# Query loads in rows of 1024 bytes, with two schedules reordered, in a retention kernel followed by a low-rank mixer

## The chip, the cores and the metric

The kernel runs on one core of one Trainium2 chip. The metric is the device time of one execution in microseconds; lower is better. A core has a matrix engine (TensorE, "PE" in the profile, with its weight loads as "PEld"), a vector engine (DVE), an activation engine (ACT), a general engine (POOL) and a small engine whose queue issues DMAs (SP). Each takes its instructions in the order in which the program gave them; semaphores let one wait for another. Sixteen DMA engines move the data of all queues.

## The reference

Four batches (B), eight heads (H), 768 tokens (S), 64 numbers to a head (D). A recurrent attention with a decay per head is followed by a mixer: a low-rank mixing of the tokens (rank 32), then an MLP of 512 -> 2048 -> 512.

```python
gamma = 1.0 - 2.0 ** (-5.0 - np.arange(H, dtype=np.float32))
scale = 1.0 / np.sqrt(D)
for t in range(S):
    state = gamma[None, :, None, None] * state + np.einsum('bhd,bhe->bhde', k[:, :, t], v[:, :, t])
    y[:, :, t] = scale * np.einsum('bhd,bhde->bhe', q[:, :, t], state)
...
x = np.ascontiguousarray(attn_out.transpose(0, 2, 1, 3)).reshape(B, S, H * D)
...
h = xt @ U @ V                      # xt: x with tokens and features exchanged
u = x + h.transpose(0, 2, 1)
ch = np.maximum(u @ w_ch1, 0.0) @ w_ch2
return (u + ch).astype(np.float32)
```

## The kernel before, in words

**Attention in chunks.** The recurrence is turned into matrix products. A chunk has 128 tokens, so a batch has six (NCK). Scores of a chunk are k times q, masked to the past; outputs are masked scores times v plus q times the state of the chunks before. The decay enters as factors exp(position x log gamma): positive powers go with q, negative ones with k or v. `gq`, `gk` hold them one token to a partition, `gq2`, `gk2` two tokens to a partition. The factor of q can be put on q when it is cast to bf16, or on the output x.

**Batch 0 and its units.** Batch 0 works in six units: unit u has four heads (g = 0 or 1) and 256 tokens (one of three blocks). `load_heads` (line 105) brings a unit in with two neighbouring tokens on each partition: for each partition and head a row of 2 x 64 x 4 = 512 bytes. The loads are issued on SP in the order of the list in line 115, and land in a ring of 20 buffers (`ring`, line 97). What happens to them is an order written out by hand, `STEPS`: K0, Q0, V0 are the casts to bf16 of unit 0, Tk0 and Tq0 the transposes on TensorE (as matmuls with the identity), kT0 and qT0 their way out of PSUM, S0 the scores, m0 the mask, ST0.0 a chunk's addition to the state and s0.0 its copy, M0 the mix, x0 the output; FTk1:3 are three matmuls with zeros that keep TensorE busy. `BY` says for each unit which engine (A, D, P for ACT, DVE, POOL) does a step, whether q is `scaled` in its cast, and whether the negative power goes on k (`ks` = 1) or v. If q is not scaled, `x_out` multiplies on DVE. The last steps (xt, P, pc, E, N, R, u, B) are the low-rank mixing and the first MLP matmuls (`begin_up`, line 400).

**Weights.** The step w0 makes POOL copy one element of the last q unit (line 746, the gate), so that the first quarter of w1 is loaded only after it; w1 is the second quarter. After `STEPS`, POOL issues the third quarter and, behind `feed_behind(511)`, the fourth, then four loads for w2, and stands before `feed_behind(1023)`. `feed_behind(col)` copies an element of w1 that arrives with the first or second quarter into a ring buffer; SP's next load into that buffer has to wait for it.

**Feed of batches 1 to 3.** `feed` lists the loads in order; `feed_more` issues them while ring buffers are free and `n_open` allows: two at first, six behind the first gate, the rest of batch 1 behind the second. k and v of batch 1 come one token to a partition, in rows of 256 bytes; q of batch 1 comes like batch 0's units.

**MLP passes with the next batch woven in.** `mlp_pieces(b)` gives a batch's MLP as pieces: 16 up-projections of 512 tokens (line 429), 8 of the other 256 tokens for two blocks each (line 442), then the down-projections (line 458). Each up-projection fills one of three PSUM banks called `mlp`, and a relu on ACT or, every third time, on DVE empties it (lines 420 and 418). `weave` emits the pieces in order and, before them, the steps of the next batch's attention whose mark, a share of the pass, has come: `turn_k1`, `turn_q1` (transposes of batch 1 into `mlp` banks, with an evacuation each), `score`, `mix`, the casts `prep_two`, and the low-rank steps. `score` masks on DVE (line 284), `mix` uses the state from `nsz`. Outputs are stored from POOL's queue (line 408).

## Time and profile before

| | us |
|---|---|
| median of three runs | 226.52 |
| the three runs | 229.25, 224.36, 226.52 |
| the profiled execution | 223.51 |
| its span, first to last instruction | 221.7 |
| TensorE busy in the span | 216.1 |
| matmuls of line 458 / 429 / 442 | 88.1 / 56.8 / 29.6 |
| relus on ACT (line 420) / DVE (line 418) | 38.1 / 22.1 |

The profile was taken in one execution. A busy time is the sum of an engine's instructions, and a group's mean is that of one instruction. The chain is followed back from the last instruction: at each step to what released it, or to the instruction before it on its engine. In timelines the columns are the start, the time taken, the engine, line, operation, and output and input with partitions x elements; in brackets the idle time before it and what ended it. Where the DMA engines and TensorE stand in the span's 40 equal slices of 5.5 us:

```profile
DMA  5999999999999996789896644411112530001112
GB/s 163 317 303 253 189 219 203 195 217 229 306 261 263 279 269 108 166 174 211 168 295 167 174 122 97 95 43 31 47 52 88 152 95 0 0 3 47 72 70 96
DMA packets 89381, 34.58 MB, mean 156 GB/s; under 512 B 71216, under 2 KB 87856, under 8 KB 89360
```

The DMA engines are busy in 9 tenths or more of the first 80 us or so, TensorE nearly everywhere.

### The profile page before, as it was taken

How to read it: one execution, taken by the hardware profiler on the slowest of the kernel's cores; microseconds unless marked ns; L12 is line 12 of the kernel's file. 1: busy time of each engine (PE TensorE's matmuls, PEld its weight loads, DVE VectorE, ACT ScalarE, POOL GpSimd, SP SyncE). 2: the span in 40 equal slices, each digit the busy share in tenths (PEclk: the TensorE clock that was granted, in tenths of full speed). 3: DMA queues.
4: the chain of work that ended last, by engine and by line, in shares of the span. 5: the costliest groups of instructions: out<-in, count | busy, mean ns of one | idle time of the engine just before them, and what ended most of it. 6: DMA issues, size and time to landing. Idle time of an engine off the chain costs nothing.

```text
span 221.7 us, 4773 instructions
## 1 busy us (share of the span) xinstructions
PE 216.1 (97%) x1982; PEld 122.9 (55%) x1982; DVE 96.7 (44%) x137; ACT 82.6 (37%) x157; POOL 79.3 (36%) x114
## 2 busy tenths in 40 slices
PE   7999999999999999999999999999999999999994
PEld 2567444775665544588454444587454444774442
DVE  6578546226445266526336144443525242221121
ACT  3676354454554134484230034746030044430000
POOL 5589473126760059390100498530101000000110
PEclk9999999999999999999999999999999999999999
DMA  5999999999999996789896644411112530001112
GB/s 163 317 303 253 189 219 203 195 217 229 306 261 263 279 269 108 166 174 211 168 295 167 174 122 97 95 43 31 47 52 88 152 95 0 0 3 47 72 70 96
DMA packets 89381, 34.58 MB, mean 156 GB/s; under 512 B 71216, under 2 KB 87856, under 8 KB 89360
## 3 DMA queue, kind: packets, MB, share of 16 engines
q1 hardware_dynamic: 83296, 24.06, 47.1%
q0 software_dynamic: 6064, 10.23, 18.6%
q8 instruction: 15, 0.25, 0.4%
q14 instruction: 6, 0.05, 0.1%
HBM read 27.46 MB, written 6.29 MB: 152 GB/s over the span
## 4 chain that ended last, share of the span: by engine, by line
PE 87%; SPq 6%; DMA 5%; issue 0%; ACT 0%; DVE 0%; POOL 0%
PE mlp L458 38%; PE mlp L429 25%; PE mlp L442 13%; SPq L106 5%; DMA w1b<-in_moe_w_ch_dram 3%; PE r L281 2%; PE r L302 2%; DMA in<-in_q_dram 2%; PE r L297 2%; PE st L313 2%; PE r L344 1%; PE mlp L400 1%; PE mlp L271 1%; PE r L382 0%; SPq L117 0%
## 5 line engine op out<-in xcount | busy, mean ns | idle before, releaser
L458 PE MATMUL mlp<-w2b,gT 128*128 128x512 bf16 (+2 forms) x400 | 88.1, 371 | 0.0
L420 ACT ACTIVATE gT<-mlp 128x512 bf16<-128x512 f32 x64 | 38.1, 597 | 70.2 <-PE mlp L429 57.4
L458 PEld LDWEIGHTS <-gT 128*128 128x128 bf16 x400 | 36.9, 98 | 38.6 <-issue 0.2
L429 PE MATMUL mlp<-uT,w1b 128*128 128x512 bf16 x250 | 56.8, 379 | 0.0
L408 POOL DMA_DIRECT2D out_dram<-o x23 | 12.7, 554 | 103.5 <-DVE o L465 95.8
L418 DVE TENSOR_SCALAR gT<-mlp 128x512 bf16<-128x512 f32 x32 | 22.1, 690 | 46.2 <-PE mlp L429 23.9
L429 PEld LDWEIGHTS <-w1b 128*128 128x128 bf16 x250 | 23.6, 98 | 27.3
L465 DVE TENSOR_TENSOR o<-mlp,u 128x512 f32<-128x512 f32 (+2 forms) x25 | 16.8, 670 | 45.0 <-PE mlp L458 44.8
L442 PE MATMUL mlp<-uT,w1b 128*128 128x256 bf16 x256 | 29.6, 273 | 0.2 <-ACT gT L420 0.2
L442 PEld LDWEIGHTS <-w1b 128*128 128x128 bf16 x256 | 24.8, 98 | 4.2 <-issue 0.4
L284 DVE TENSOR_TENSOR a<-r,mask 128x1024 bf16<-128x1024 f32 x18 | 21.2, 1219 | 7.0 <-PE r L281 7.0
L83 POOL TENSOR_TENSOR vd<-in,gk 128x512 bf16<-128x512 f32 x18 | 18.7, 1040 | 10.4 <-DMA in<-in_v_dram 10.2
L70 ACT ACTIVATE x<-r 128x512 bf16<-128x512 f32 x20 | 11.9, 596 | 25.9 <-PE r L302 25.6
L351 DVE TENSOR_TENSOR u<-r,x 128x512 bf16<-128x512 f32 (+1 forms) x16 | 14.6, 951 | 3.9 <-PE r L344 3.9
L81 POOL CAST kd<-in 128x512 bf16<-128x512 f32 x16 | 9.7, 611 | 8.0 <-issue 6.2
L83 POOL TENSOR_TENSOR qd<-in,gq 128x512 bf16<-128x512 f32 x12 | 12.5, 1041 | 0.0
L70 ACT ACTIVATE nsz<-st 64x256 bf16<-64x256 f32 x30 | 11.2, 372 | 0.3
L83 POOL TENSOR_TENSOR qp<-in,gq 128x512 bf16<-128x512 f32 x6 | 6.2, 1052 | 5.6 <-DMA in<-in_q_dram 5.6
L591 DVE TENSOR_TENSOR a<-r,mask 128x1024 bf16<-128x1024 f32 x6 | 7.3, 1222 | 2.0 <-PE r L584 2.0
L302 PE MATMUL r<-vd,a 128*128 128x64 bf16 x144 | 7.1, 193 | 0.0
L302 PEld LDWEIGHTS <-a 128*128 128x128 bf16 x144 | 6.0, 98 | 0.7
L297 PEld LDWEIGHTS <-qT 128*128 128x128 bf16 x60 | 4.6, 98 | 2.7
(109 smaller groups left out, 152.2 us busy)
## 6 DMA issues: line engine op xcount, KB each, us to landing
in<-in_k_dram SPq DMA_DIRECT2D x24, 256.0 KB, 4.9
in<-in_q_dram SPq DMA_DIRECT2D x24, 256.0 KB, 4.7
in<-in_v_dram SPq DMA_DIRECT2D x24, 256.0 KB, 4.8
out_dram<-o POOLq DMA_DIRECT2D x23, 256.0 KB, 2.3
w1b<-in_moe_w_ch_dram POOLq DMA_DIRECT2D x4, 512.0 KB, 8.7
w2b<-in_moe_w_ch_dram POOLq DMA_DIRECT2D x4, 512.0 KB, 15.8
kT<-kd SPq DMA_TRANSPOSE x12, 2.4
qT<-qd SPq DMA_TRANSPOSE x12, 2.4
```

The lines of the kernel that those rows point to most:

```text
L70: nc.scalar.activation(dst, src, AF.Copy)
L83: e.tensor_tensor(dst, src, scale, op=ALU.mult)
L284: nc.vector.tensor_tensor(a, r.rearrange("p i (n m) -> p i n m", n=4), mask[:, None, None, :].to_broadcast([P, 2, 4, P]), op=ALU.mult)
L302: nc.tensor.matmul(o[:, ts(h, D)], a[:, i, hp], vb[:, h], start=(ci == 0 and h == 0), stop=True, skip_group_check=True)
L351: nc.vector.tensor_tensor(v4(us[b][:, ds(j0, nj), e]), R[g][:, :, :nj * P].rearrange("p c (j e) -> p c j e", j=nj), v4(xs[b][:, ds(j0, nj) ...
L408: eng.dma_start(out=dst, in_=src)
L418: nc.vector.tensor_relu(dst, src)
L420: nc.scalar.activation(dst, src, AF.Relu)
L429: nc.tensor.matmul(g_p[:, :sz], w1b[:, c, ts(m, P)], uTs[b][:, c, ds(lo, sz)], start=(c == 0), stop=(c == NCB - 1))
L442: nc.tensor.matmul(g_p[:, ts(n, S - LO)], w1b[:, c, ts(m + n, P)], uTs[b][:, c, LO:], start=(c == 0), stop=(c == NCB - 1))
L458: nc.tensor.matmul(ch[:, :nn], gT[:, m, ts(j, P)], w2b[:, m, ds(n0, nn)], start=(m == 0), stop=(m == NM - 1))
L465: nc.vector.tensor_tensor(o_sb, ch[:, :nn], us[b][:, j, n], op=ALU.add)
```

## The change

q of batches 0 and 1 is loaded with four neighbouring tokens on a partition, in rows of 1024 bytes. A q unit is now one of three parts of a group g of four heads: parts 0 and 1 hold two heads and 512 tokens each, part 2 holds four heads and the last 256 tokens, in two loads of 64 partitions. A score unit therefore needs two q units (0 and 1, or 3 and 4) or part 2 alone. The transposed q of a whole batch goes to one tile (`qT0`, or the one of batch 1), written with a step of four elements. q of batch 0 is no longer scaled in its cast, so all six outputs x are multiplied on DVE, and `gq2` goes. Batch 1's q is scaled by new constants `g4`, made by `q4_consts`, which is called after `feed_behind(1023)`. The order of batch 0's loads, its `BY` and its `STEPS` are new; so are the feed's order for q of batch 1 and the marks of its transposes and of its first k casts.

```diff
+    Q4 = 512
+    def load_q4(t, b, i):
+        g, part = divmod(i, 3)
+        if part < 2:
+            nc.sync.dma_start(
+                out=t.rearrange("p (h x) -> p h x", h=2),
+                in_=q[b, ds(HG * g + 2 * part, 2), ds(0, Q4), :].rearrange(
+                    "h (t j) d -> t h (j d)", j=4))
+            return
+        for n in range(2):
+            nc.sync.dma_start(
+                out=t[ds(64 * n, 64)].rearrange("p (h x) -> p h x", h=2),
+                in_=q[b, ds(HG * g + 2 * n, 2), ds(Q4, S - Q4), :].rearrange(
+                    "h (t j) d -> t h (j d)", j=4))
...
-    for step in ("k0 q0 v0 k1 q1 v1 k2 q2 v2 k3 q3 v3 k4 q4 U k5 q5 v4 v5 ").split():
+    for step in ("k0 q0 q1 v0 k1 v1 k2 q2 v2 k3 q3 q4 v3 k4 U k5 q5 v4 v5 ").split():
...
-    feed = [(nm, 1, 2 * pp + n) for pp in range(NCK // 2) for nm in "kqv"
-            for n in range(2)]
+    QS = ((0, 1, 3, 4), (), (2, 5))
+    feed = [(nm, 1, ci) for pp in range(NCK // 2) for nm in "kqv"
+            for ci in (QS[pp] if nm == "q" else (2 * pp, 2 * pp + 1))]
...
-    gq2 = consts.tile([P, NB, H, 2], fp32)
-    nc.scalar.activation(gq2, pos2, AF.Exp)
...
-    nc.vector.tensor_scalar(gq2, gq2, 1.0 / math.sqrt(D), None, op0=ALU.mult)
...
+    g4 = consts.tile([P, H + 4, 4], fp32)
+    def q4_consts():
+        pa, pc = ramp([P, H, 4], [[0, H], [1, 4]], 4), ramp([P, 4, 4], [[0, 4], [1, 4]], 4, Q4)
+        nc.vector.tensor_scalar(pc[ds(64, 64)], pc[ds(64, 64)], -256.0, None, op0=ALU.add)
+        nc.vector.tensor_tensor(
+            g4[:, :H], pa, lgt[:, :, None].to_broadcast([P, H, 4]), op=ALU.mult)
+        lgv = lgt.rearrange("p (g n h) -> p n g h", n=2, h=2)
+        for n in range(2):
+            r = ds(64 * n, 64)
+            nc.vector.tensor_tensor(
+                g4[r, H:].rearrange("p (g h) j -> p g h j", g=2),
+                pc[r].rearrange("p (g h) j -> p g h j", g=2),
+                lgv[r, n, :, :, None].to_broadcast([64, 2, 2, 4]), op=ALU.mult)
+        nc.scalar.activation(g4, g4, AF.Exp)
+        nc.vector.tensor_scalar(g4, g4, 1.0 / math.sqrt(D), None, op0=ALU.mult)
...
+    def cast_q4(eng, b, i, src, scaled):
+        t = rpre.tile([P, 4, 2, D], bf16, tag="qd", name=f"q4_{b}_{i}")
+        cast(eng, t, src.rearrange("p (h j d) -> p j h d", h=2, j=4),
+             scale_q4(i) if scaled else None)
+        return t
+    def turn_q4(tp, t):
+        for j in range(4):
+            nc.tensor.matmul(tp[:, ts(j, P)], t[:, j], ident, start=True, stop=True)
+    def turned_q4(eng, qT, i, tp):
+        g, part = divmod(i, 3)
+        if part < 2:
+            evac(eng, qT[:, 2 * g + part, :Q4].rearrange("p (t j) -> p j t", j=4),
+                 tp.rearrange("p (j t) -> p j t", j=4))
+        else:
+            evac(eng, qT[:, ds(2 * g, 2), Q4:].rearrange("p n (t j) -> p j n t", j=4),
+                 tp.rearrange("p (j n t) -> p j n t", j=4, n=2))
...
     def prep_two(nm, pp, eng="P"):
-        for ci in (2 * pp, 2 * pp + 1):
+        for ci in QS[pp] if nm == "q" else (2 * pp, 2 * pp + 1):
...
-        evac("AD"[g], t[:, ds(2 * g, 2)].rearrange("p n (t j) -> p n j t", j=2),
-             tp.rearrange("p (n j t) -> p n j t", n=2, j=2))
+        tp = bank("mlp")
+        turn_q4(tp, pre.pop(("q", 1, i)))
+        turned_q4("ADADAD"[i], bts["q1"], i, tp)
...
-             "K": "DDPPPP",
-             "Q": "PPDPPA",
-             "scaled": "111000",
-             "ks": "110010",
-             "V": "APPPPP",
-             "kT": "AADAAA",
-             "qT": "AAAAAA",
-             "x": "AADDAD",
+             "K": "DPPPPP",
+             "Q": "ADPPPA",
+             "scaled": "000000",
+             "ks": "101011",
+             "V": "APAPPP",
+             "kT": "DAADAA",
+             "qT": "ADAAAA",
+             "x": "DDDDDA",
...
-        "Va K0 Vb FTk0:1 Q0 Tk0 FTq0:2 Vc V0 Tq0 kT0 ST0.0 FTk1:3 K1 qT0 Tk1 Q1 "
-        "s0.0 S0 kT1 ST0.1 FTq1:1 m0 V1 s0.1 Tq1 qT1 K2 ST1.0 M0 s1.0 S1 Q2 x0 "
-        "ST1.1 Tk2 m1 s1.1 V2 Tq2 FTk3:2 qT2 K3 ST2.0 kT2 M1 s2.0 Q3 S2 x1 Tk3 "
-        "m2 V3 Tq3 FTk4:2 kT3 qT3 ST3.0 K4 M2 s3.0 S3 x2 Q4 Tk4 ST3.1 Ub m3 Tq4 "
-        "FTk5:3 kT4 K5 qT4 s3.1 Tk5 w0 Q5 M3 S4 kT5 x3 Tq5 V4 xt0 qT5 m4 w1 "
-        "ST4.0 xt1 s4.0 S5 V5 ST4.1 m5 M4 s4.1 P0 x4 ST5.0 M5 s5.0 pc0 N5 E0 x5 "
-        "P1 u1 xt2 R2 xt3 u0 pc2 E2 E3 u2 B1 u3 B2 "
+        "Va Q0 K0 Vb FTk0:1 Tk0 FTq0:2 Q1 Vc Tq0 FTq1:2 V0 kT0 Tq1 qT0 ST0.0 "
+        "FTk1:3 qT1 K1 s0.0 Tk1 V1 S0 kT1 ST0.1 m0 s0.1 S1 K2 ST1.0 s1.0 m1 M0 "
+        "Q2 Tk2 V2 ST1.1 Tq2 x0 M1 FTk3:1 kT2 K3 s1.1 x1 Tk3 qT2 Q3 ST2.0 kT3 "
+        "Tq3 Q4 s2.0 S2 qT3 Tq4 FTk4:4 m2 V3 qT4 ST3.0 K4 S3 s3.0 M2 Ub m3 K5 "
+        "Tk4 ST3.1 kT4 x2 M3 w0 Q5 Tk5 s3.1 S4 kT5 x3 Tq5 V4 xt0 qT5 m4 w1 "
+        "ST4.0 xt1 s4.0 S5 V5 ST4.1 m5 M4 s4.1 ST5.0 P0 s5.0 x4 M5 pc0 N5 E0 x5 "
+        "P1 u0 xt2 R2 xt3 u1 pc2 E2 E3 u2 B1 u3 B2 "
...
     feed_behind(1023)
+    q4_consts()
     for t in nsz:
         nc.gpsimd.memset(t, 0.0)
     for nm in "kqv":
         prep_two(nm, 0)
...
+    Q1_AT = (0.49, 0.49, 0.52, 0.52, 0.755, 0.755)
...
-                mark(pair_at - dt[1], turn_q1, ci)
...
-            for nm, eng, at in (("k", "AP", (0.51, 0.635)), ("q", "PP", (0.54, 0.67)),
+            for nm, eng, at in (("k", "AP", (0.535, 0.635)), ("q", "PP", (0.54, 0.67)),
                                 ("v", "PP", (0.58, 0.70))):
...
+            for at, i in zip(Q1_AT, (0, 1, 3, 4, 2, 5)):
+                mark(at, turn_q1, i)
```

In batch 1, q was turned before at 0.045 of the pass ahead of each pair of score chunks, which stand at 0.565, 0.685 and 0.80.

## The prediction

> **What bounds the kernel now.** I read the page first: TensorE is busy for 97% of the span, and only the first tenths of the second row are not at 9.
>
> ```profile
> PE 216.1 (97%) x1982; PEld 122.9 (55%) x1982; DVE 96.7 (44%) x137; ACT 82.6 (37%) x157; POOL 79.3 (36%) x114
> PE   7999999999999999999999999999999999999994
> ```
>
> Then the chain that ended last, in order of time (start, length, what):
>
> ```profile
> 13.99 3.75 DMA in<-in_q_dram
> 17.74 0.05 issue
> 17.79 0.12 POOL gate L746
> 17.91 7.46 DMA w1b<-in_moe_w_ch_dram
> 25.38 0.05 issue
> 25.42 1.47 PE mlp L400 x6
> 26.89 0.43 PE mlp L429 x2
> 27.32 0.22 PE r L344 x8
> 27.54 2.70 PE mlp L429 x12
> ```
>
> Before 25.42 us the kernel is paced by loads: q's last unit, the gate behind it on POOL, then the first quarter of w1. From 25.42 on the chain is TensorE almost without a hole, to the end. So 196 us can only get longer by a hole in TensorE, and only the first 25.4 us can get shorter. TensorE had finished batch 0's part by 25.10 (its last matmul of L682 starts at 24.71 and takes 0.39), so w1 came 0.3 us after it was needed. That the loads are paced by the DMA engines shows in the stretches (engine busy times, clock, DMA share, GB/s):
>
> ```profile
> 5.50:11.00 5.50, 5.19 (x78) 3.13 (x78) 3.09 (x4) 3.77 (x8) 3.01 (x4) 1.00 1.07 316
> 11.00:17.70 6.70, 6.40 (x166) 4.68 (x163) 5.28 (x7) 4.92 (x11) 5.38 (x7) 1.00 1.09 304
> ```
>
> The share is at 1 or above: there is always a packet waiting. Last, the timeline around 25 us for the three engines that serve TensorE:
>
> ```profile
> 25.43 0.18 POOL L764 CAST in<-w1b 1x1 f32<-1x1 bf16 x1 [3.24 <-DMA w1b<-in_moe_w_ch_dram]
> 25.56 0.74 POOL L229 DMA_DIRECT2D w1b<-in_moe_w_ch_dram  x1
> 26.29 2.98 POOL L234 DMA_DIRECT2D w2b<-in_moe_w_ch_dram  x4
> 29.23 0.17 POOL L764 CAST in<-w1b 1x1 f32<-1x1 bf16 x1
> 29.35 1.44 POOL L778 MEMSET nsz<- 128x512 bf16 x3
> 25.74 0.68 DVE L72 CAST uT<-r 128x512 bf16<-128x512 f32 x1
> 27.58 1.29 DVE L351 TENSOR_TENSOR u<-r,x 128x512 bf16<-128x512 f32 x2 [1.16 <-PE r L344]
> 28.79 0.68 DVE L418 TENSOR_SCALAR gT<-mlp 128x512 bf16<-128x512 f32 x1
> 27.14 1.09 ACT L420 ACTIVATE gT<-mlp 128x512 bf16<-128x512 f32 x2 [2.58 <-PE mlp L429]
> ```
>
> Two things: POOL waits for the first quarter of w1 and then issues five weight loads before it comes to the line behind `feed_behind(1023)` at 29.40; and ACT and DVE empty the first three up-projection banks (m = 0, 1 on ACT, 2 on DVE) from 27.14 on. Every engine keeps the program's order: L778's memset needs no data and still stands behind both gates.
>
> **The change, part by part.**
>
> *Row length of q.* In the trace's packet records between 2 and 16 us a 512 B packet takes 27 ns, one of 3072 B 121 ns; between 18 and 25.4 us one of 256 B takes 18 ns. By the line from 512 to 3072, 1024 B takes 27 + 94 x 512/2560 = 46 ns. A load of 512 packets over 16 engines costs 32 x 27 = 864 ns, one of 256 packets 16 x 46 = 736 ns: 0.13 us each, and six stand ahead of the gate: -0.8 us. Ends: 0 (the packets are cut to 512 B) and -1.1 (the gate reads partition 0, so it may wait for the first half of unit 5 alone, 0.37 us less). All that follows the gate (7.46 us of w1 beside the last loads, the same bytes) moves with it: -0.8.
>
> [...]
>
> *Two half loads for units 2 and 5.* One more issue each on SP's queue, by the row of 0.5 us for a free issue. SP is ahead of the engines (unit 5 is issued at 13.99 and lands at 17.74), so nothing; up to +0.5 if that lead were gone.
>
> *Batch 0's order and sides.* TensorE's matmuls are the same but for 13 filling ones in place of 14. q is never scaled in the cast: two POOL casts of 1.05 and one of 0.69 on DVE become 0.61 to 0.69 on ACT, DVE and POOL. The first three outputs x, copied by ACT, ACT and DVE, become multiplications of 0.69 on DVE. With K1 gone to POOL (-0.69) and one more kT and qT (0.68, 0.73), DVE's sum before 25.4 us, 17.8 by the stretches, grows to 17.8 + 2 x 0.69 - 0.69 + 0.68 + 0.73 = 19.9, still short of full. The transposed q is written with a step of four: rows with a step of two took 744 ns against 592 without, so 0.74 to 0.9. The last steps, from V4 on, are the same but for the places of ST5.0, P0 and u. I take 0, between -0.5 and +1: up to about 3 us of lateness is covered by the wait below, and without that wait it is paid beyond 0.3 + 0.8. The first scale's removal (ACT 0.24, DVE 0.19) lies under k0's load, for which DVE waited 0.78.
>
> *The new constants, `q4_consts`.* Here is the cost. POOL makes two ramps behind `feed_behind(1023)`; DVE has four small operations on them; ACT an Exp; DVE one more. In program order all of them precede the first relu. So DVE, done with uT at 26.42, and ACT, done before that, stop until POOL is there. From its rows: POOL reaches the ramps at 29.40. Seven ramps took 1.55 at the start, so two 0.45: 29.85. Four DVE operations of 0.15 to 0.19 (L171, L186): about 30.50. ACT's Exp on 48 columns 0.24 (L188): 30.75. The first relu 0.60: TensorE gets its first bank back at 31.35. Meanwhile TensorE fills the three banks (m = 0, 1, 2) and would start m = 3 at 27.54 + 0.86 = 28.40. The hole is 31.35 - 28.40 = 2.95 us (2.6 to 3.3 by the spread of these small rows). Next in line behind it: DVE's last scale 0.19, u 1.29, relu of m = 2 until about 32.9, wanted at 31.35 + 2 x 0.86 = 33.07: just in time. Since POOL's chain hangs on the same quarter of w1 as TensorE's start, the -0.8 moves both: the net here is -0.8 + 2.95. No second table load: the one at 0.73 serves Exp, Copy and Relu alike.
>
> *A colder clock after the hole.* The first nine matmuls of 512 columns took 4.02 us, 0.44 each; later ones in the chain take 2.70/12 = 0.22. If the hole brings that back, four microseconds at half speed lose 2.0. No hole above 0.4 us stands in this trace once it is warm, so it shows neither; bounds 0 and +2.0. I take 0 by the nearest row: a pause of 0.62 before the weight load at 5.89, after which three matmuls of 512 columns took 0.82 at 7.94 (0.27 each), so the clock rose through it.
>
> [...]
>
> *Batch 1.* SP's order becomes q0 q1 q3 q4 v0 v1. Four loads of 256 packets are as many packets as two of 512, and beside the weights (60% of packet time in 25 to 60 us) the loads advanced packet by packet: v0 and v1 are cast near 43.6 and 48.6 as before, for a first use at 55.03 (L302). v0 also stands behind the second gate now, long open (29.4). w2's last quarter gets some 1024 x 19 ns/16 = 1.2 us later, and the hole delays its use by more. POOL's six casts stay at 1.05.
> Four transposes at 0.49 and 0.52 of the pass in place of two at 0.52: the first down-projection then takes the bank of the last up-projection, whose relu on DVE ends at 48.50 + 0.69 = 49.19, while TensorE, done with that up-projection at 47.42 + 1.03 = 48.45 and with two transposes of 0.22 each, is free at 48.90: +0.25, rounded (0 to 0.8, should more evacuations be late). The k casts that move on ACT from 0.51 to 0.535 of the pass had to wait for their loads (1.12 of idle time); 0.
>
> **Sum.** -0.8 + 2.95 + 0.25 = +2.4 us. The profiled execution took 223.51 (span 221.7, 1.8 around it): 225.9. It is 3.0 under the median of the runs, 226.52; there it is 228.9, which I forecast.
>
> **Rivals.**
> *The constants are covered (faster).* If POOL reached the ramps before TensorE ran out of banks, the hole is gone and -0.8 + 0.25 = -0.55 stays: 226.0. It decides below 28.40 - 1.95 = 26.45 for POOL, 3 us before what its rows show; against it stands the memset at 29.35.
> *The clock falls after the hole:* +2.4 + 2.0 = 4.4: 230.9. Decided by whether a pause of 3 us is enough.
> *The rows are not really longer:* packets remain 512 B, or the halves cost what the rows give. Then +3.2 to +3.7: 229.9. DMA packet counts of the page decide.
>
> **How the numbers follow.** Forecast 0.60, covered 0.14, clock 0.17, rows 0.09. 2% (4.5 us) is about what a measurement of this kernel can tell from no change: below 222.0 or above 231.05. The runs spread from 224.36 to 229.25, so -2.2 and +2.7 about the median. Slower by over 2%: half of the clock case and somewhat more, 0.10, a quarter of the rows case, 0.02, and a fifth of the forecast (hole 3.3, turns 0.8, a high draw), 0.12: 0.24. Faster by over 2% needs the covered case and a low draw: 0.05. The rest 0.71. The range runs from just under the covered case, 225.4, to just above the clock case, 231.6.
>
> **What would show it.** Right: a pause of about 3 us on TensorE some 3 us after its first L400, ended by ACT's relu; ACT's Exp waiting on DVE and DVE on a POOL ramp; unit 5 landing near 16.9. Wrong: no such pause; matmuls of 0.44 after it (clock); a packet count that falls by less than 12 x 256 = 3072 from 89381 (rows); TensorE's start of L400 later than 25.4 (batch 0's order).

## The result, and the profile after

The changed kernel took 233.38 us (median of four runs, 231.06 to 233.93) and the kernel before, on the same chip, 225.84 (224.36 to 229.25): a ratio of 1.034, 95% interval 1.023 to 1.045. It is slower, by more than the forecast of 228.9 and by more than the end of its range, 231.6. The medians here and below hold all executions of a kernel; the ratios and their intervals leave out those that took over 1.5% longer than its fastest.

The profiled execution of the changed kernel took 233.93 us (span 232.2), against 223.51 (221.7) before: 10.4 us more. The medians lie 7.5 apart; the other 2.9 come from which executions were profiled (2.3 under the median before, 0.55 over it after). On the page, the rows that answer to those of before:

```profile
PE 218.2 (94%) x1981; PEld 123.0 (53%) x1981; DVE 102.5 (44%) x144; ACT 85.3 (37%) x155; POOL 78.4 (34%) x115
...
PE   7788756999999999999999999999999999999994
...
PEclk9999997999999999999999999999999999999999
...
DMA packets 86374, 34.59 MB, mean 149 GB/s; under 512 B 71280, under 2 KB 84848, under 8 KB 86352
...
L484 PE MATMUL mlp<-uT,w1b 128*128 128x512 bf16 x250 | 58.3, 386 | 4.8 <-ACT gT L475 4.8
```

TensorE is no longer busy throughout: the first seven slices (5.8 us each) are at 5 to 8 tenths, and in the seventh the clock was granted at 7 tenths. After that the row is all nines, as before. There are 3007 packets fewer. The prediction's sign against longer rows was a fall of less than 12 x 256 = 3072; by the rows' parts the packets from 512 B up to 2 KB fall by just 3072 (16640 to 13568), and 64 of the missing 65 are packets under 512 B, of which there are more. So the rows are longer, as the change says. The last row gives TensorE 4.8 us of idle time in one place, before an up-projection (L484; it was L429 before). Marks of the program split the span; both columns add up to their span:

| from, to (us) | before | after | difference |
|---|---|---|---|
| start, batch 0's first up-projection | 25.42 | 28.95 | +3.53 |
| that, its first down-projection | 22.87 | 30.10 | +7.23 |
| that, batch 1's first up-projection | 30.45 | 30.12 | -0.33 |
| batch 1's pass | 49.35 | 49.35 | 0 |
| batch 2's pass | 48.46 | 48.46 | 0 |
| batch 3's pass and the end | 45.19 | 45.19 | 0 |

So there are two places: the start, and batch 0's pass. The chain of waits after passes through both (start, length, what):

```profile
13.63 5.68 DMA in<-in_k_dram
...
19.47 1.05 POOL ku L83
20.52 0.07 POOL gate L803
20.59 8.31 DMA w1b<-in_moe_w_ch_dram
...
32.91 0.27 POOL ramp L170 x2
33.18 0.02 issue
33.21 1.96 DVE ramp L216
35.16 0.03 issue
35.20 0.55 DVE g L217
35.74 0.09 DVE g L222
35.86 0.18 DVE g L222
36.04 0.02 issue
36.06 0.24 ACT g L226
36.30 0.49 ACT gT L475
36.80 0.04 issue
36.84 3.21 PE mlp L484 x8
```

The upper lines are the start: a load of k that lands at 19.31, POOL's cast of this unit (K5), a gate at 20.52 (17.79 before), and a first quarter of w1 that takes 8.31 (7.46 before). K5 stands ahead of the gate in POOL's queue. The change moves the negative power of unit 5 from v to k (`ks`, last digit), so K5 is now a multiplication of 1.05 us and no longer a cast of 0.62. The gate's own load, q's last unit, had landed by then (its halves at 19.93 and 20.21). The lower ones are `q4_consts`, a link at a time: POOL's ramps, DVE's four operations, ACT's Exp, the first relu, and only then TensorE. One of DVE's operations, on 64 partitions of 16 numbers, takes 1.96 us. The timeline sets what POOL does beside it (start, time taken, engine, line, and so on as before):

```profile
33.13 1.45 POOL L838 MEMSET nsz<- 128x512 bf16 x3
33.21 1.96 DVE L216 TENSOR_SCALAR ramp<-ramp 64x16 f32<-64x16 f32 x1 [3.67 <-POOL ramp L170]
34.53 1.16 POOL L81 CAST kd<-in 128x512 bf16<-128x512 f32 x2
...
36.84 3.21 PE L484 MATMUL mlp<-uT,w1b 128*128 128x512 bf16 x8 [4.80 <-ACT gT L475]
```

DVE's operation began 0.08 after POOL's memsets, lasted through all three and into the two casts (of 0.58 each), and ended near the end of the first; the next one (0.55 from 35.20 on) ended near the end of the second. TensorE's hole is 4.80, and its next eight matmuls take 3.21 us, 0.40 each; in the kernel before, at a clock of 1.00, matmuls of this form start 0.216 apart (L429), which makes 8 x 0.216 = 1.73.

The stretches last (engine busy times, clock, DMA share, GB/s):

```profile
5.50:11.00 5.50, 4.21 (x55) 2.29 (x55) 3.10 (x4) 2.41 (x5) 0.70 (x2) 1.00 1.05 273
11.00:17.70 6.70, 5.59 (x134) 3.83 (x125) 5.22 (x6) 5.08 (x10) 5.14 (x7) 1.00 1.05 262
36.00:41.00 5.00, 4.16 (x20) 1.84 (x20) 2.01 (x5) 2.73 (x6) 3.13 (x3) 0.66 1.18 239
```

In the first two the DMA engines are as full as before, at a share over 1, and move 273 and 262 GB/s in place of 316 and 304. Their packets take longer, though fewer are sent: one of 512 B takes 34.8 ns on average between 8 and 14 us, against 27.5 before. The prediction has no term for that. The third shows the clock after the hole: 0.66.

### The profile page after: what moved, and what is told of

It is laid out like the page before. It is cut to its first block, busy times and chain, and to the rows that moved or that the text cites. A ratio compares the mean times of both kernels' runs of the same rounds, so it can differ in the third digit from the quotient of the medians.

```text
span 232.2 us, 4777 instructions
## 1 busy us (share of the span) xinstructions
PE 218.2 (94%) x1981; PEld 123.0 (53%) x1981; DVE 102.5 (44%) x144; ACT 85.3 (37%) x155; POOL 78.4 (34%) x115
## 4 chain that ended last, share of the span: by engine, by line
PE 82%; DMA 9%; SPq 2%; POOL 2%; DVE 2%; ACT 1%; issue 1%; POOLq 0%
PE mlp L513 36%; PE mlp L484 24%; PE mlp L497 12%; DMA in<-in_k_dram 6%; DMA w1b<-in_moe_w_ch_dram 4%; PE r L336 2%; PE r L357 2%; PE st L368 1%; PE r L352 1%; SPq L106 1%; POOL w2b L295 1%; PE r L399 1%; DVE ramp L216 1%; ACT gT L475 0%; POOL ku L83 0%
## 5 line engine op out<-in xcount | busy, mean ns | idle before, releaser
L484 PE MATMUL mlp<-uT,w1b 128*128 128x512 bf16 x250 | 58.3, 386 | 4.8 <-ACT gT L475 4.8
L484 PEld LDWEIGHTS <-w1b 128*128 128x128 bf16 x250 | 23.9, 99 | 33.2 <-issue 6.8
L520 DVE TENSOR_TENSOR o<-mlp,u 128x512 f32<-128x512 f32 (+2 forms) x25 | 16.7, 669 | 46.6 <-PE mlp L513 46.6
L70 ACT ACTIVATE x<-r 128x512 bf16<-128x512 f32 x18 | 10.7, 596 | 25.5 <-PE r L357 25.2
L81 POOL CAST kd<-in 128x512 bf16<-128x512 f32 x16 | 9.7, 608 | 10.4 <-issue 8.0
L70 ACT ACTIVATE qT<-mlp 128x512 bf16<-128x512 f32 x8 | 10.3, 1325 | 1.3 <-PE mlp L243 1.2
L83 POOL TENSOR_TENSOR q<-in,g 128x512 bf16<-128x512 f32 x6 | 6.3, 1060 | 3.2 <-DMA in<-in_q_dram 2.2
## 6 DMA issues: line engine op xcount, KB each, us to landing
w2b<-in_moe_w_ch_dram POOLq DMA_DIRECT2D x4, 512.0 KB, 16.9
```

The costliest lines, as they stand in the source:

```text
L70: nc.scalar.activation(dst, src, AF.Copy)
L83: e.tensor_tensor(dst, src, scale, op=ALU.mult)
L484: nc.tensor.matmul(g_p[:, :sz], w1b[:, c, ts(m, P)], uTs[b][:, c, ds(lo, sz)], start=(c == 0), stop=(c == NCB - 1))
L520: nc.vector.tensor_tensor(o_sb, ch[:, :nn], us[b][:, j, n], op=ALU.add)
```

## The experiments

The ratios are to the kernel before, with 95% intervals; 1% is 2.25 us. "Start" is the start of batch 0's first up-projection.

**The hole: its place, its cover and the clock.** Four kernels move or fill the constants' wait. The first is the kernel before with nothing but the constants, unused, at the place where the change has them:

```diff
     feed_behind(1023)
+    q4_consts()
```

> The kernel before with q4_consts added at the place where the change has it; nobody reads its result. Theory: the same hole, 4.5 to 5 us, opens behind the first three up-projections, the clock falls for some 4 us, and the kernel before becomes 6 to 6.5 us longer, near 232. Rival (it takes the late loads of the change to open the hole): within 1 us of the kernel before.

232.72 us, ratio 1.032 (1.026 to 1.038): this edit alone loses nearly all that the change loses. Its timeline, and its stretches of 31 to 36 and 36 to 41 us:

```profile
30.91 1.44 POOL L796 MEMSET nsz<- 128x512 bf16 x3
30.99 1.96 DVE L196 TENSOR_SCALAR ramp<-ramp 64x16 f32<-64x16 f32 x1 [3.64 <-POOL ramp L147]
...
34.63 3.57 PE L446 MATMUL mlp<-uT,w1b 128*128 128x512 bf16 x8 [4.83 <-ACT gT L437]
```

```profile
31.00:36.00 5.00, 1.37 (x4) 0.53 (x4) 4.63 (x8) 1.22 (x3) 3.53 (x6) 0.72 1.19 210
36.00:41.00 5.00, 5.00 (x22) 2.35 (x21) 0.62 (x2) 2.22 (x3) 1.05 (x1) 0.60 1.21 197
```

The hole is 4.83 and the same 1.96 stands in it. From its start (26.71) to batch 1's first up-projection it took 60.93 us, against 53.32 before: +7.61, of which 4.83 is the hole and 2.8 what follows it at a clock of 0.60 to 0.72. The unused constants also move the buffers that the loads land in, of which more below; the start is 1.29 later here.

Next, the changed kernel with the constants made at the start of the program:

```diff
     late_consts()
+    q4_consts()
     open_x(0)
...
     feed_behind(1023)
-    q4_consts()
```

> The changed kernel with q4_consts called at the start, behind late_consts, in place of behind feed_behind(1023); nothing else. Theory (the constants' place in the queues makes the hole, and the hole lets the clock fall): the hole of 4.80 us on TensorE before the fourth up-projection is gone, the granted clock stays at 1.00, and 6.3 us of the loss go: some 227 us, 2.5 to 4 above the kernel before. Rival (TensorE would have had to wait there anyway, for weights or for late loads): the hole stays or moves by a few us, and the time stays near 233.

230.05 us, ratio 1.015 (1.006 to 1.025). The hole is gone: from 31.42 on TensorE's up-projections follow one another, and start to first down-projection is 23.95 in place of 30.10. The same three operations of DVE, with POOL at rest, take 0.17, 0.19 and 2 x 0.18:

```profile
4.39 0.17 DVE L216 TENSOR_SCALAR ramp<-ramp 64x16 f32<-64x16 f32 x1
4.60 0.19 DVE L217 TENSOR_TENSOR g<-ramp,lgt 128x32 f32<-128x32 f32 x1
...
4.71 0.36 DVE L222 TENSOR_TENSOR g<-ramp,lgt 64x16 f32<-64x16 f32 x2
```

But the start came at 29.98, not at 25.42: DVE's first cast of k waited behind the constants (5.48 in place of 4.76), and TensorE, with more waits in the first stage, ran at a clock of 0.50 from 11.00 to 17.70 (not in every execution: the shortest, 228.24 us, had 1.00 throughout). So the hole was not the whole of the loss.

Third, the changed kernel with the three memsets of `nsz` taken from POOL to ACT at the start, so that only casts follow the ramps on POOL:

```diff
     late_consts()
+    for t in nsz:
+        nc.scalar.activation(t.rearrange("p n m -> p (n m)"), zeros, AF.Copy)
...
-    for t in nsz:
-        nc.gpsimd.memset(t, 0.0)
```

> The changed kernel with the three zero fills of nsz moved from POOL (behind the ramps) to copies on ACT at the start. Theory (DVE's first operation on the ramps, 1.96 us long for 64 x 16 numbers, waits for the POOL instructions that run beside it): with only the two casts of k behind the ramps it takes 0.6 to 1.2 us, and the hole shrinks from 4.80 to 3.4 to 4.0 us. Rival (the operation itself is slow, for its place in the upper 64 partitions): it stays at 1.96 and the hole at 4.8.

One execution, 231.49 us. The hole is gone, and L216 takes 0.17 again. It doesn't tell what was asked: the clock fell in the first stage (to 5 tenths in the page's slices from 23 to 34 us), TensorE started at 31.10, and POOL had made the ramps at 30.51, before that start; DVE came to L216 at 32.52, when POOL's casts were over. Inconclusive on the memsets; the 0.17 agrees with the run above.

Fourth, the changed kernel with 20 matmuls on zeros put into the hole:

```diff
+    def warm():
+        t = bank("st")
+        for _ in range(20):
+            nc.tensor.matmul(t, zeros[:, :P], zeros, start=True, stop=True)
+    pieces0.insert(3, (0.0, warm))
```

> The changed kernel with 20 matmuls of zeros (4.3 us of TensorE at the full clock) put behind the third up-projection, into a bank that nobody uses then. Theory (the slow 36 to 41 us come from the clock, which falls because TensorE stands still for 4.8 us): the hole is filled but for half a us, the clock stays at 1.00, the 8 matmuls after it take 1.7 in place of 3.2 us, and the kernel is 1.5 us shorter, near 232. Rival (the slow matmuls wait for w1): the clock's row changes, those 8 matmuls stay at 3.2 us and the time stays.

231.94 us, ratio 1.028 (1.022 to 1.034). Its timeline around the hole:

```profile
30.86 4.48 PE L898 MATMUL st<-zeros 128*128 128x512 bf16 x20
...
31.30 1.45 POOL L838 MEMSET nsz<- 128x512 bf16 x3
31.37 1.40 DVE L216 TENSOR_SCALAR ramp<-ramp 64x16 f32<-64x16 f32 x1 [2.19 <-POOL ramp L170]
...
35.18 1.89 PE L484 MATMUL mlp<-uT,w1b 128*128 128x512 bf16 x8
```

The eight matmuls behind it take 1.89 us in place of 3.21, and the clock, 0.66 from 36 to 41 us in the changed kernel, is 1.00: it was the idleness that cost the clock. Start to first down-projection is 28.27, 1.83 less than without the zeros, of which 1.32 is these eight. The ratio's interval overlaps that of the change, so in whole times the gain isn't told apart.

**The rows of q.** The kernel before with q of batch 0 loaded as in the change, in its old order and places. The transposes stay, so batch 0's scores see q's tokens in another order:

```diff
+        if nm == "q":
+            load_q4(t, 0, u)
+        else:
+            load_heads(t, src_of[nm], 0, *UNITS[u])
```

> The kernel before with its six q units of batch 0 loaded as in the change (rows of 1024 B, units 2 and 5 in two loads of 64 partitions), at their old places in the order; all else as before, so that q's numbers stand at other tokens and heads than the steps take them for. Theory L (the longer rows or the half loads slow the loading): the first matmul on w1, at 25.42 us in the kernel before, comes at 27.5 to 29, and the time grows by 2 to 3.5 us. Rival S (the new order of batch 0's steps and loads does it): it comes at 24.6 to 25.4, as the packet rows of the kernel before promise, and the time is 0 to 0.8 shorter.

Ratio 1.001 (0.998 to 1.003). The forecast's -0.8 us would be 0.9964, outside the interval: in this form the rows gain nothing.

The same with one whole load for every q unit, to be rid of the halves (units 4 and 5 read again what 0 and 1 read, so the numbers of q are others):

```diff
+    def load_q4(t, b, i):
+        nc.sync.dma_start(
+            out=t.rearrange("p (h x) -> p h x", h=2),
+            in_=q[b, ds(2 * (i % 4), 2), ds(0, 512), :].rearrange(
+                "h (t j) d -> t h (j d)", j=4))
```

> The kernel before with all six q units of batch 0 loaded in rows of 1024 B over 128 partitions, none in halves (two heads, the first 512 tokens; units 4 and 5 read what 0 and 1 read). The steps take other numbers for q than the reference's. If the long rows are slow: the first matmul on w1 as late as with the halves (27.5 or more). If the half loads are slow: back to 24.6 to 25.4.

Ratio 0.999 (0.995 to 1.003), start at 26.08. The stretches show that the rows do what was priced:

```profile
5.50:11.00 5.50, 4.73 (x82) 2.92 (x81) 3.23 (x4) 3.83 (x8) 3.03 (x4) 1.00 1.04 314
11.00:17.70 6.70, 6.19 (x154) 4.51 (x151) 5.34 (x7) 5.04 (x10) 5.15 (x7) 1.00 1.06 316
```

316 GB/s against 304 in the second stretch, and in the packet records 46.3 ns for 1024 B and 27.0 for 512 between 8 and 14 us: the forecast's 46 and 27. Yet unit 5's last part lands at 17.9 (17.7 before). Half of the sixteen DMA engines have their parts done by 16.7 (17.1 before), fifteen by 16.9, and the last at 17.9. But an earlier landing of this load alone would have gained nothing either: ahead of the gate POOL has K5's cast, which started here when TensorE's transposes let it (17.3; its own load landed at 17.2). The last links before the gate in this kernel, and K5 in the kernel before:

```profile
17.34 0.62 POOL ku L81
17.96 0.09 POOL gate L755
```

```profile
17.12 0.62 POOL L81 CAST ku<-in 128x512 bf16<-128x512 f32 x1 [0.24 <-DVE x L72]
```

In the kernel before the cast and q's last load both end at 17.74. So the packets are shorter, and neither the load nor the cast lets the gate come earlier. The interval reaches down to 0.995 and doesn't exclude the forecast's 0.9964 for whole loads; no trace here shows that gain.

Then the halves alone, in rows of 512 B:

```diff
+        if nm == "q" and u in (2, 5):
+            for n in range(2):
+                nc.sync.dma_start(
+                    out=t[ds(64 * n, 64)].rearrange("p (h x) -> p h x", h=HG),
...
```

> The kernel before with units 2 and 5 of q in two loads of 64 partitions each, rows of 512 B as before and the same numbers in the same places. If the half loads are slow: the first matmul on w1 at 26.5 or later. If the long rows are: 25.4 within 0.4, and the time of the kernel before.

225.76 us, ratio 1.007 (1.004 to 1.009), start at 26.70. This is 1.5 us for the two halves, where 0 to 0.5 had been set. k's last unit lands at 17.73 (16.97 before), K5's cast follows it, and the gate comes at 18.49 in place of 17.79, with q's last half landed at 18.48. In that profile the clock was also at 0.50 for 3.4 us from 26.45 on; the four other executions had 1.00 and took 225.3 to 225.9, so the ratio isn't the clock's.

And the changed kernel with its q loads cut into rows of 512 B, two loads for one:

```diff
+            for a in range(2):
+                nc.sync.dma_start(
+                    out=t.rearrange("p (h a x) -> p h a x", h=2, a=2)[:, :, a],
...
```

> The changed kernel with each q load split into two, one for each half of a row, so that the packets have 512 B as before while units, order and steps stay those of the change. If the long rows are slow: the first matmul on w1, at 28.95 in the changed kernel, comes at 27 or earlier, and the time falls by 2 or more from 233. If the order of batch 0 is slow: it stays at 28.5 to 29.5 and the time near 233.

234.65 us, ratio 1.047 (1.042 to 1.052), start at 33.67. The 4.7 us by which it starts later are not the loads': POOL's gate comes at 20.6 (20.5 in the changed kernel) and the first quarter of w1 is there at 29.3 (28.95), but the clock was at 0.50 from 15.81 to 36.29, and TensorE itself was late. So this is no clean test of the rows. It shows no more than that rows of 512 B don't give back what the change loses.

**Batch 0's order, sides and evacuations.** The new order of the loads in the kernel before:

```diff
-"k0 q0 v0 k1 q1 v1 k2 q2 v2 k3 q3 v3 k4 q4 U k5 q5 v4 v5 "
+"k0 q0 q1 v0 k1 v1 k2 q2 v2 k3 q3 q4 v3 k4 U k5 q5 v4 v5 "
```

> The kernel before with batch 0's loads in the order of the change (q1 ahead of v0, q4 ahead of v3), units, rows and steps as before. If that order slows the loading itself: unit 5 of q lands at 19 us or later (17.7 in the kernel before) and the time grows by 1.5 or more. If not: 17.5 to 18.5, and the time within 1 us.

Ratio 1.001 (0.997 to 1.005), start at 26.11: nothing. The reverse, the old order of the loads in the changed kernel with its constants at the start:

```diff
-"k0 q0 q1 v0 k1 v1 k2 q2 v2 k3 q3 q4 v3 k4 U k5 q5 v4 v5 "
+"k0 q0 v0 k1 q1 v1 k2 q2 v2 k3 q3 v3 k4 q4 U k5 q5 v4 v5 "
```

> The changed kernel with the constants at the start (the run of that kind took 1.015 of the kernel before, its first matmul on w1 came at 29.98 us), and with batch 0's loads in the order of the kernel before (q1 behind k1, q4 behind k4); steps and q units as changed. If the order of the loads holds the first stage up: the first matmul on w1 comes at 26 to 27.5, and the time at 1.000 to 1.006 of the kernel before. If the steps do it (the transposed q is written with a step of four, 1.3 us each on ACT and DVE in place of 0.74): it stays at 28.5 or later and the time at 1.012 or more.

228.85 us, ratio 1.023 (1.019 to 1.027), start at 29.25. The kernel it differs from had 1.015 (1.006 to 1.025): the intervals overlap, and no gain shows.

All of batch 0's part and nothing of batch 1's: `load_q4`, the order of the loads, `BY`, `STEPS` and the transposed q of the change; no new constants, `gq2` as it was.

```diff
-             "scaled": "111000",
+             "scaled": "000000",
...
-        "Va K0 Vb FTk0:1 Q0 Tk0 FTq0:2 Vc V0 Tq0 kT0 ST0.0 FTk1:3 K1 qT0 Tk1 Q1 "
+        "Va Q0 K0 Vb FTk0:1 Tk0 FTq0:2 Q1 Vc Tq0 FTq1:2 V0 kT0 Tq1 qT0 ST0.0 "
...
+    qT0 = open_qT(0)
...
```

> The kernel before with batch 0's part of the change alone: its loads, their order, units, steps and engines; batch 1 and its constants as before. Theory (the first stage's 3.5 us are real and come from batch 0's part): the first matmul on w1 at 27.5 us or later, the time 1.008 to 1.018 of the kernel before. Rival (they were the profiled execution's own): 25.4 to 26.5 and 0.997 to 1.005.

224.94 us, ratio 1.004 (1.001 to 1.007): +0.9 us. In its profile k's last unit lands at 17.73, K5 takes POOL 1.05 us from 17.89 on, and the gate comes at 18.93, 1.14 later than before. The same with the transposed q written contiguously (so batch 0's tokens of q stand in another order):

```diff
-            evac(eng, qT[:, 2 * g + part, :Q4].rearrange("p (t j) -> p j t", j=4),
-                 tp.rearrange("p (j t) -> p j t", j=4))
+            evac(eng, qT[:, 2 * g + part, :Q4], tp)
...
```

> The same with the transposed q of batch 0 written side by side, so that q's tokens stand in another order than the scores take them for. If the evacuations of 1.3 us hold the first stage up: 1.5 us or more shorter than with the step of four. If the loads do: within 0.7 us of it.

224.57 us, ratio 1.002 (0.999 to 1.004). The group of these evacuations on ACT, first with the step of four, then contiguous (count, busy time, mean ns):

```profile
L70 ACT ACTIVATE qT<-mlp 128x512 bf16<-128x512 f32 x5 | 6.4, 1338 | 0.0
```

```profile
L70 ACT ACTIVATE qT<-mlp 128x512 bf16<-128x512 f32 x5 | 3.0, 594 | 0.1
```

1.34 us against 0.59, and the forecast had 0.74 to 0.9. It costs little here; the two intervals overlap. The same edit in the changed kernel with its constants at the start:

```diff
-            evac(eng, qT[:, 2 * g + part, :Q4].rearrange("p (t j) -> p j t", j=4),
-                 tp.rearrange("p (j t) -> p j t", j=4))
+            evac(eng, qT[:, 2 * g + part, :Q4], tp)
...
```

> The changed kernel with the constants at the start, and with the transposed q of batches 0 and 1 written side by side (no step of four), so that q's tokens stand in another order than the scores take them for. If these evacuations hold the first stage up: they take 0.6 in place of 1.3 us, the first matmul on w1 comes at 26 to 27.5, and the time at 1.000 to 1.006 of the kernel before. If the loads and their order do it: 28.5 or later, 1.012 or more.

227.75 us, ratio 1.016 (1.010 to 1.022), against 1.015 with the step: no difference.

**Batch 1's part alone.** First with the constants at the start: the kernel before with the change's feed, constants, casts and transposes for batch 1.

```diff
+    q4_consts()
     open_x(0)
...
-                mark(pair_at - dt[1], turn_q1, ci)
...
+            for at, i in zip(Q1_AT, (0, 1, 3, 4, 2, 5)):
+                mark(at, turn_q1, i)
```

> The kernel before with batch 1's part of the change alone (its loads, feed order, casts, transposes and their marks, and the constants, made at the start); batch 0 as before. Theory: +0.3 us for the waits among the transposes, 1.000 to 1.004 of the kernel before; so the rest of the 1.015 belongs to batch 0. Rival: batch 1's longer evacuations and later v hold TensorE up, 1.01 or more.

226.50 us, ratio 1.012 (1.010 to 1.015), start at 26.96. Then with the constants split, so that neither the start nor the pass waits for them: POOL makes the ramps in the first stage, after V1b, and the rest comes at 0.13 of batch 0's pass, with batch 1's first casts behind it.

```diff
+            nc.gpsimd.tensor_copy(out=V1b, in_=V1)
+            return q4_ramps()
...
-    q4_consts()
...
+    mark(0.13, prep_first)
```

> The kernel before with batch 1's part of the change alone, and the constants in the two places of the first run of this set in place of the start. Theory (of the 1.0124 of batch 1 alone, 0.75 us are its transposes and the rest the constants at the start, which delay the first cast of k): 1.002 to 1.006. Rival (batch 1's part itself costs 2 us or more): 1.009 or more.

226.83 us, ratio 1.010 (1.005 to 1.016), start at 27.45. Start to first down-projection took 23.82 (22.87 before) and from there to batch 1's first up-projection 30.12 (30.45): +0.62 for the transposes that were moved. Where they stand:

```profile
50.52 0.69 DVE L475 TENSOR_SCALAR gT<-mlp 128x512 bf16<-128x512 f32 x1 [2.77 <-PE mlp L499]
50.74 1.31 ACT L70 ACTIVATE qT<-mlp 128x512 bf16<-128x512 f32 x1 [0.37 <-PE mlp L245]
51.12 1.29 DVE L72 CAST qT<-mlp 128x512 bf16<-128x512 f32 x1
51.26 1.02 PE L515 MATMUL mlp<-w2b,gT 128*128 128x512 bf16 x3 [0.34 <-DVE gT L475]
```

TensorE waits 0.34 for DVE's relu (the forecast had 0.25), and in all 0.8 in front of the down-projections. But the start is 2 us late, and nothing of batch 1 stands before it. The constants split in the same way in the whole change:

```diff
+            return q4_ramps()
...
-    q4_consts()
...
+    mark(0.13, prep_first)
```

> The changed kernel with the constants taken out of both bad places: the two ramps behind POOL's cast of V at the start, DVE's and ACT's part at 0.13 of batch 0's pass. Theory (hole and clock are the constants', the rest is the first stage and batch 1's waits): no hole, and the time at 1.012 to 1.022 of the kernel before (3.5 us of the first stage, 0.75 of batch 1). Rival (the constants are nearly all of it, and the run with the constants at the start was slow for their place there): 1.000 to 1.008.

228.57 us, ratio 1.018 (1.008 to 1.027). No hole, clock 1.00, start to first down-projection 23.82, and a start at 28.43. In whole times this is 1.6% (3.6 us) less than the change, where hole and clock together are 6.3 us in the profiles. With intervals of about 1% on both ratios the difference lies between 0.4 and 6.8 us, so the two don't contradict each other, but the size of the hole's part rests on the traces.

**The place of the ring.** What the late starts have in common shows in the packet records, set beside the place of the input ring in each program. The pool of the constants lies ahead of the weights and the ring. The change takes `gq2` away (192 B to a partition) and adds two ramps (128 and 64) and `g4` (192): the ring starts 192 B later. In the kernel before it starts at a multiple of 256 B. Mean time of a 512 B packet between 8 and 14 us:

| ring's start beyond a multiple of 256 B | kernels | 512 B packet, ns |
|---|---|---|
| 0 | before and those with the rows, halves, loads or all of batch 0 alone | 27 to 30 |
| 128 | constants in the kernel before, batch 1 alone (both) | 32.6 to 33.6 |
| 192 | the change, and the kernels made from it so far | 35 to 42 |

Two runs were made of this. The kernel before with an unused tile of 192 B, and nothing else:

```diff
     zeros = consts.tile([P, 512], bf16)
+    pad = consts.tile([P, 48], fp32)
```

> The kernel before with one unused tile of 192 B to a partition among its constants and nothing else: every tile behind it, the input ring and the weights among them, starts 192 B later, so that a ring buffer starts 192 B behind a multiple of 256 B, as in the changed kernel; in the kernel before it starts at a multiple of 256 B. Theory (placement): the rows of the loads now straddle these bounds, so the 512 B packets between 8 and 14 us take 32 to 38 ns on average and not 27.5, the loads move 265 to 295 GB/s there and not 323, TensorE's first up-projection starts at 26.5 to 28.5 us and not at 25.4, and the time is 1.005 to 1.014 of before. Rival (the placement is indifferent; the loads were slowed by the constants' instructions or by the order of the steps): 27 to 28 ns, first up-projection at 25.4 to 26.2, ratio 0.998 to 1.003.

228.24 us, ratio 1.011 (1.007 to 1.015). The packets take 33.8 ns; the stretches:

```profile
5.50:11.00 5.50, 5.21 (x84) 2.98 (x82) 2.87 (x3) 3.74 (x8) 3.05 (x4) 1.00 1.17 298
11.00:17.70 6.70, 5.75 (x148) 3.99 (x142) 4.84 (x7) 4.21 (x9) 4.75 (x6) 1.00 1.16 271
```

Same instructions, same loads, other addresses: 298 and 271 GB/s in place of 316 and 304. The unused tile moves all that lies behind the constants, the weights too; the 512 B packets between 8 and 14 us go to the ring. The start in the profile, 26.11, lies below what was expected (26.5 to 28.5); this execution was the kernel's shortest (225.54), and two kernels with the ring in its place start no earlier in their profiles (26.08 and 26.11, above). So the loss is shown by the packets, the rates and the whole times, not by this start. The profile lost 1.2 us more in batch 1's pass, where TensorE waits 1.04 for a transposing DMA of the next batch's q; with whole q loads and the ring in its place it waits 0.77 there, so this wait isn't shown to be the ring's.

The whole change with split constants, and 64 B of padding that put the ring at a multiple of 256 again:

```diff
     zeros = consts.tile([P, 512], bf16)
+    pad = consts.tile([P, 16], fp32)
```

> The changed kernel with its constants split as in e1_consts_split (no hole), and one unused tile of 64 B to a partition among its constants, so that its ring starts at a multiple of 256 B again. Theory (placement): between 8 and 14 us the 512 B packets come back from 36 ns to 27 to 29 and the 1024 B ones from 59 to 46 to 53; the first up-projection starts at 25.9 to 27.2 us and not at 28.43. What stays is the pass (0.95 - 0.33 + 0.68 = +1.3 us, 0.6%) and up to 0.4% from batch 0's steps: ratio 1.004 to 1.011 of before, against 1.0176 with the ring off by 192 B. Rival (indifferent): packets and start as in e1_consts_split, ratio 1.014 to 1.021.

225.84 us, ratio 1.006 (1.003 to 1.009), where the same without the padding had 1.018. Packets 27.9 and 47.8 ns, start 26.32 in place of 28.43:

```profile
5.50:11.00 5.50, 4.48 (x78) 2.69 (x76) 4.00 (x5) 3.02 (x5) 2.62 (x4) 1.00 1.13 337
11.00:17.70 6.70, 5.63 (x123) 3.77 (x123) 5.20 (x8) 5.80 (x9) 4.84 (x8) 1.00 0.95 282
```

With the hole and the shift both gone, most of the loss is gone. None of these kernels beats the kernel before by more than its interval; this one is the change at its best.

## Why the prediction was wrong, point by point

**The hole (right in kind, too small).** Chain, place and order were as forecast: POOL reached the ramps 3.92 us after TensorE's first up-projection (forecast 3.98), and ACT's relu ended the wait. The term that failed is "Four DVE operations of 0.15 to 0.19". They took from 33.21 to 36.04, 2.83 us in place of 0.65, and the hole 4.80 in place of 2.95 (the other terms came 0.3 shorter together). The early constants show the forecast's durations for the same operations; the difference is what POOL does beside them. The trace of before had a row that said so: DVE's mask took 0.98 beside a cast on POOL,

```profile
2.80 0.98 DVE L173 TENSOR_SCALAR mask<-ramp,ramp 128x256 bf16<-128x256 f32 x1
2.81 0.81 POOL L691 CAST V1b<-V 32x768 bf16<-32x768 f32 x1 [0.43 <-DMA V<-in_moe_V_dram]
```

and 0.39 in the kernel with early constants, where no cast lay beside it. That kernel has the reverse too: a multiplication of 128x48 on DVE took 0.81 beside the cast, and one of the same size 0.21 without it. The forecast took its durations from rows with no memset or cast of POOL's beside them, and itself put the memset right behind the ramps. In these rows DVE's operations take longer beside POOL's; why they do, and why this one lasted through several of POOL's instructions, no run shows.

**The clock (failed).** "I take 0 by the nearest row": it was 3.21 - 1.73 = 1.48 us. The rival "the clock falls after the hole" was right, with 2.0 for it, but was tied to a hole of 2.95. The zeros in the hole kept the clock at 1.00, which shows the cause. How long a hole may be isn't shown: here are holes of 4.80 and 4.83 and none of 3. In the traces' records the clock fell to 0.50 some 4.1 us after TensorE's last matmul in the changed kernel (at 36.13, for 3.41 us) and 3.4 us after it in the kernel before with the constants. A hole of 2.95 would have ended before either, so the 0 may have failed only because the hole was longer than the forecast's; with no shorter hole in any run this stays an estimate.

**The rows (failed).** The packet times were right and the -0.8 was not. The step that failed is "six stand ahead of the gate: -0.8 us": the gate stands behind K5's cast in POOL's queue, which ended at 17.74 in the kernel before, together with the load that the prediction names, and at 17.96 with whole loads; and the last of the sixteen DMA engines, at 17.9, kept nothing of the saving. The rows alone gave 1.001 (0.998 to 1.003). In the changed kernel the gate doesn't wait for q at all, but for k's last load and the cast behind it.

**The loads' start address (missing).** No term of the sum stood for it; the new constants were priced by their instructions alone, not by the 192 B by which they move all that lies behind them. Alone it costs 1.1% (0.7 to 1.5), 2.4 us. It is what "TensorE's start of L400 later than 25.4" was to warn of, though that line put it down to batch 0's order. In the profiled executions the start came 3.53 later; putting the ring back took off 2.1 of the 3.0 in the kernel without the hole, and 1.2% in whole times.

**Batch 0's order and sides.** 0, with -0.5 to +1, was set; all of batch 0 alone gave +0.9 us (0.1 to 1.7). Inside the bounds; the evacuations were mis-sized (1.34 us, not 0.74 to 0.9), without much effect. What the list of casts leaves out is K5 on POOL, 1.05 us in place of 0.62 just ahead of the gate; in the profile of this part alone the gate comes 1.14 later, the longer cast being 0.43 of that.

**The half loads.** 0 to +0.5 was set; alone in rows of 512 B they cost 1.5 (1.0 to 2.0). With long rows beside them they don't show.

**Batch 1.** +0.25 (0 to 0.8) was set for the transposes; +0.62 by the stages. The 0.34 at the bank of the last up-projection is the forecast's 0.25. What makes the rest isn't shown: batch 1's part alone has further waits of 0.05 to 0.16 in front of its down-projections, the changed kernel has none, and both come to +0.62.

The parts of batch 0's pass close: 4.80 + 1.48 + 0.62 = 6.90, which is the table's 7.23 - 0.33. For the start they don't: 2.4 for the ring, 0.9 for batch 0's part are averages of runs, and 3.53 is one execution. In whole times the loss falls from 1.034 to 1.018 without the hole and to 1.006 with the ring put back: steps of 3.6 and 2.7 us, and 1.3 that stay.

## What to carry to other kernels

Before pricing an edit that adds or removes a constant, work out which tiles it moves. Here the loads of the first stage ran best into buffers at a multiple of 256 B (27.5 and 27.9 ns for a 512 B packet, against 33.8 at 192 B past it), and 64 B of padding took the ratio from 1.018 to 1.006: where loads pace a kernel, such padding is worth a run. Price a small vector operation by a row that has the same neighbour on POOL, not by one that stands alone (1.96 us beside three memsets and a cast, 0.17 alone), and put constants where no engine has work queued behind them: here they made a hole of 4.80 us. The saving in packet time (46 ns for 1024 B, where two of 512 B take 54) came to nothing, with a ratio of 0.999 for whole loads: the last of the sixteen DMA engines was done at 17.9 us (17.7 before), and a cast of 0.62 us stood in POOL's queue ahead of the gate. Look at both before counting on such a saving.

## What the runs showed of the hardware that was not expected

- *The start address of a load's target.* Rows of 512 B into buffers that start 192 B past a multiple of 256 B: 33.8 ns for a packet in place of 27.5, 23% more, the same program otherwise; at 128 B past, 32.6 to 33.6, in kernels that differ in more; back at a multiple of 256 B, 27.9 in the changed kernel with split constants and padding. The target moved and the source didn't; why the packets take longer isn't shown.
- *DVE against several POOL instructions.* One operation of 0.17 us (constants at the start) took 1.96 beside three memsets and a cast (the changed kernel), and 1.40 beside three memsets (with zeros in the hole): by the profile several of POOL's instructions went by before it ended.
- *The clock.* 0.72 and 0.60 in the stretches 31 to 36 and 36 to 41 us, in and after a hole of 4.83 (the kernel before with the constants), 0.66 from 36 to 41 after one of 4.80 (the changed kernel), and 1.00 where zeros filled it. It fell without such a hole too: in the profile with early constants it was 0.50 from 11.00 to 17.70, after a stretch (5.50 to 11.00) in which TensorE was busy for 3.19 of 5.50 us and waited 0.89 at the longest. The changed kernel, busy for 4.21 of the same 5.50 us, kept 1.00 there and in the next stretch.
- *Strided writes of bf16.* ACT out of PSUM, 128x512: 0.59 us contiguous (batch 0's part with plain evacuations), 0.74 with a step of two (the kernel before), 1.34 with a step of four (batch 0's part alone).
